# A fused attention and snake-MLP kernel on one core: softmax sums of the first chunk moved from TensorE to VectorE, and new plans for the stages

## The chip, the cores and the metric

The kernel runs on one core of a Trainium2 chip. The metric is the device time of one launch in microseconds (us). Five engines of the core work side by side, each through its own queue in order: TensorE (PE in the profile, with PEld for its weight loads), VectorE (DVE), ScalarE (ACT), GpSimd (POOL) and SyncE (SP), which here issues transfers. They wait for each other by semaphores.

## The reference, cut to what matters

Attention over 8 batches, 12 heads, 448 positions and head size 64, with q and k normalised to unit mean square; its output, laid out as 3584 rows of 768, goes through two matrix products with a "snake" function between them.

```python
q_n, k_n = rmsnorm(q, g_q), rmsnorm(k, g_k)          # q, k, v: (8, 12, 448, 64), float32
scores = (1 / sqrt(64)) * q_n @ k_n.T
attn = exp(scores - max) / (sum(exp) + 1e-9)
x = (attn @ v).transpose(0, 2, 1, 3).reshape(3584, 768)
h = x @ w_in                                         # 768 -> 2048
g = h + sin(alpha * h) ** 2 / alpha
out = g @ w_out                                      # 2048 -> 768
```

## The kernel before

**Stages.** The program is unrolled over the 8 batches; a batch is a stage `b`. A stage first does attention and then the first product (`first_product`, L401). The second product of batch `b - 1` (`quadrants`, L480) is cut into small fillers, which stand in TensorE's queue between the pieces of attention of batch `b`. The last second product stands alone at the end (`whole_array`, L461).

**Chunks.** The 12 heads of a batch are three chunks of four heads: chunk 0, 1 and 2 of stage `b` are `3b`, `3b+1`, `3b+2`. For each chunk, q and k are loaded (L158, L161), squared (`square`: ACT at L262 for the first two chunks, later POOL at L265), summed over the head (`reduce`, DVE, L271), turned into `1/rms` (`rsqrt`, ACT, L280 and L281), multiplied by the gains (`fold_g`, POOL, L268), scaled (`scale`, L290: DVE for chunks 0 to 3 of the whole program, later POOL) and transposed (`pe_transpose` with TensorE at L313 in the first stages, `transpose` by DMA later).

**Scores.** The 448 keys are seven tiles of 64. One `S` makes the scores of one tile for the four heads of a chunk: four 64x64 matmuls that run side by side in the four quarters of TensorE (L335), then one exponential on ScalarE (L338) from the PSUM tile `sc` to a tile `expT` of 128 partitions by 2x448 bf16 in SBUF. A stage has 21 `S`.

**Sums and values.** `attend` multiplies these exponentials with a block of ones ("ones", the softmax sums) and with v ("values", "low", "high"), accumulating over the seven key tiles in PSUM (`av`, L361). Chunk 0 has its own pass, "ones 0" and "values 0", with 64x64 matmuls: per key tile `2 x 2` of them, so 28 for each of the two. Chunks 1 and 2 go together with 64x32 matmuls. After the ones, ScalarE makes the reciprocal as exp(-ln(sum)) in a tile `rec` in SBUF (L366, L367), and VectorE multiplies `av` by it into `xT` (L373).

**First product.** 96 matmuls of 128x128 by 448 columns in eight PSUM tiles of two output blocks each. Each block then goes through ScalarE's sine (L379), a square (POOL at L382 for even blocks, ScalarE at L384 for odd ones) and VectorE's multiply-add into `g_sb` (L387), and only then does its PSUM tile come free.

**Fillers.** One `F` is eight 64x64 matmuls of 384 columns. After 64 of these matmuls VectorE drains the unit with a copy and an add from PSUM (L486, L487), and the PSUM tile comes free.

**Order.** All orders are written out in plans: a string of tokens for the part with attention, a string of PSUM slot numbers, and a dictionary of tasks beside the first product, keyed by its output tile (-1 is early in it, 8 its end). `STAGE_0`, `STAGE_1` and `STAGE_N` (stages 2 to 7) are such plans. Tokens: `S4` is an `S` with four idle matmuls ahead of it, `F` or a number of them fillers of the unit in work, `f` a filler of the unit after it; `o v x y z` are the passes of `attend` (ones 0, values 0, ones 1, low 1, high 1), each for so many key tiles; `q u g r k` are square, reduce, fold_g, rsqrt, scale of the chunk and half named; `p` and `t` are the transposes by TensorE and by DMA, `l V W O` loads of q and k, v, w_in, w_out, and `b` idle matmuls that keep TensorE busy. Tokens only set the order in each engine's queue. There are four PSUM tiles of two banks (`bank_pair`), shared by everything above: a matmul into a slot waits until the slot's former tile has been read.

The tile pools that matter: `expT` 17 buffers, `rec` 2, `xT` 2, `sq` 2 (of the pool `norm`), `snake` 3.

Of the kernel before, what the change touches and what calls it, by code (L numbers as in the profile page):

```python
# [17 lines left out]
try:  # L18
# [5 lines left out]
F32 = mybir.dt.float32  # L24
BF16 = mybir.dt.bfloat16
# [5 lines left out]

STAGE_0 = (
    (
        "L G b11 q00 u00 q01 g0 b15 r00 u01 k00 r01 D1 k01 V00 q11 u11 p00 q10 V02 W11 p011 S4 u10 q20 r1 "
        "g1 S4 q21 S1 l3 u20 S1 k11 k10 S4 u21 S g2 r2 p1 k20 S2 V01 S2 S o3 q30 S W00 W12 k21 l4 o4 D2 "
        "q40 W01 p2 l5 S1 g4 S u30 q31 W02 g3 u40 v1 q41 S v6 u31 S S S3 S1 S3 x2 W10 S S x1 S1 u41 x2 y2 "
        "q51 y3 x2 z1 z1 y2 z1 z1 q50 r4 r3 z2 z1 O00 k31 "
    ),
    "2122130230213212301301321032130132012120312031230",
    {-1: 'u50 k30 u51 O01', 1: 'k401 O10', 2: 'k410 k411', 3: 'O11', 4: 'V10', 5: 'k400', 6: 'D4 l6 V11', 7: 'p3', 8: 'V12 g5 l7 p4'},  # L40
)
STAGE_1 = (
    (
        "q30 6 r2 1 S 4 S 1 S 2 S 2 u30 S k21 1 q41 1 S 1 f S 1 k20 1 S 1 S 1 f 1 S 1 f f f S q31 p2 1 "
        "u31 f l5 S 2 g3 S 2 S r3 2 u41 k30 V10 S 1 q40 1 V11 q50 S o7 v7 1 S k31 1 u40 S 2 S 3 S S 1 x6 "
        "r4 k41 z2 q51 x1 t3 y7 z5 "
    ),
    "13230103120101013131312310202302301230123",
    {-1: 'g4 V12', 1: 'k40', 3: 'u50 g5', 5: 'l6 u51', 8: 't4 l7'},
)  # L50
STAGE_N = (
    (
        "1 r2 q31 q30 f 2 S V10 f 3 V11 f f k20 2 S 3 S 2 k21 S u31 q40 1 t2 1 g3 1 S 1 f u30 S 2 f S f S "
        "r3 q41 f f 1 l5 1 f S 4 u40 S S 5 S S u41 o7 v7 S S 5 S 2 q51 f S 2 S q50 k31 k30 2 S g4 1 u50 S "
        "2 r4 t3 1 S z3 x7 k40 y7 z1 z2 z1 "
    ),
    "01232302102020301301320321310130210231023",
    {-1: 'l6 u51 V12', 1: 'k41', 2: 't4 l7', 3: 'g5'},
)
LAST = "0123012"  # L60

# [1 line left out]
def tokens_of(plan):  # L63

    return [t for word in plan.split() for t in ("F" * int(word) if word.isdigit() else [word])]
# [3 lines left out]
def kernel(  # L69
# [23 lines left out]
    nc = tc.nc  # L93
    B, H, S, D = q.shape
    D_MODEL = H * D
    D_FF = moe_w_in.shape[1]
    P = 128
# [5 lines left out]
    NJ = S // REST  # L103
    assert P == 2 * REST == 2 * D
    NC = NP // 2
# [10 lines left out]
    npool = ctx.enter_context(tc.tile_pool(name="norm", bufs=2))  # L116
    tpool = ctx.enter_context(tc.tile_pool(name="qkT", bufs=8))
    epool = ctx.enter_context(tc.tile_pool(name="expT", bufs=17))
    rpool = ctx.enter_context(tc.tile_pool(name="rec", bufs=2))
    xpool = ctx.enter_context(tc.tile_pool(name="xT", bufs=2))  # L120
    gpool = ctx.enter_context(tc.tile_pool(name="g", bufs=1))
    spool = ctx.enter_context(tc.tile_pool(name="snake", bufs=3))
    opool = ctx.enter_context(tc.tile_pool(name="osb", bufs=3))
# [9 lines left out]
    def bank_pair(name, dtype=F32):  # L133
        slot = int(upcoming.popleft())
        free_at.remove(slot)
        ps = psum.tile([P, 2, 2048 // mybir.dt.size(dtype)], dtype, tag=f"ps{slot}", name=name)
        slot_of[id(ps)] = slot
        return ps

    def give_back(ps):  # L140
        free_at.append(slot_of.pop(id(ps)))
# [3 lines left out]
    def strip(c, pp, hi):  # L145

        s = 2 * hi + (pp if c == 1 else 1 - pp)
        return slice(s * 32, s * 32 + 32)
# [38 lines left out]
    ones = const.tile([P, D], BF16)  # L187
# [17 lines left out]
    def spread_g():  # L205

        nc.gpsimd.tensor_mul(g_rows[:, 2], g_rows[:, 0], g_rows[:, 1])
        ps = bank_pair("gps")
        nc.tensor.matmul(ps[:, 0, :D], ones_row, g_rows[:, 2], start=True, stop=True)  # L209
        nc.scalar.copy(gg[:, 0], ps[:, 0, :D])  # L210
        give_back(ps)

    def spread_alpha():

        ps = bank_pair("aps")
        nc.tensor.matmul(ps[:, 0, :MT], small, ident_f32, start=True, stop=True)  # L216
        nc.vector.tensor_copy(alpha_sb[:, :, 0], ps[:, 0, :MT])
        give_back(ps)
        nc.vector.reciprocal(inv_alpha_sb, alpha_sb)
# [13 lines left out]
    def load_w_out(half, part):  # L233
        src = moe_w_out.rearrange("(mt p) d -> p mt d", p=P)
        cols, mts = slice(half * HALF, (half + 1) * HALF), slice(part * MT // 2, (part + 1) * MT // 2)
        nc.gpsimd.dma_start(out=w_out_sb[:, mts, cols], in_=src[:, mts, cols])

    def keep_busy(n, rhs):


        ps = bank_pair("ps")
        for _ in range(n):
            nc.tensor.matmul(ps[:, 0, :rhs.shape[-1]], blank[:, :P], rhs, start=True, stop=True)  # L243
        give_back(ps)

    qkT, expT, xT = {}, {}, {}
# [92 lines left out]
        give_back(sc)  # L339

    avs, recs = {}, {}
    STEPS = {"o": "ones 0", "v": "values 0", "x": "ones 1", "y": "low 1", "z": "high 1"}

    def attend(b, what, tiles=range(NJ)):

        kind, both = what.split()
        both = both == "1"
        if tiles[0] == 0:  # L350
            avs[what] = bank_pair("av")
        av = avs[what]
        for j in tiles:
            for hi in range(2):
                for c in ((1, 2) if both else (0,)):
                    for pp in range(2):
                        r = slice(pp * 64, pp * 64 + 64)
                        o, k = (strip(c, pp, hi), c - 1) if both else (slice(hi * 64, hi * 64 + 64), pp)
                        d = slice(kind == "high", D, 2) if both and kind != "ones" else slice(D // 2 if both else D)
                        w = ones[r, d] if kind == "ones" else vb[b][r, 2 * c + hi, j, d]  # L360
                        nc.tensor.matmul(av[o, k, :S], w, expT[b * NC + c, j][r, hi, :], start=(j == 0), stop=(j == NJ - 1))  # L361
        if tiles[-1] < NJ - 1:
            return
        if kind == "ones":
            rec = recs[both] = rpool.tile([P, 2, S], F32, tag="rec", name="rec")
            nc.scalar.activation(rec, av[:, :, :S], ACT.Ln)  # L366
            nc.scalar.activation(rec, rec, ACT.Exp, scale=-1.0)  # L367
            give_back(avs.pop(what))
        else:
            if b not in xT:  # L370
                xT[b] = xpool.tile([P, KT, S], BF16, tag="xT", name="xT")
            kts = slice(0, 2) if not both else slice(2, KT, 2) if kind == "low" else slice(3, KT, 2)
            nc.vector.tensor_mul(xT[b][:, kts, :], av[:, :, :S], recs[both])  # L373
            give_back(avs.pop(what))
# [135 lines left out]
    def step(b, token):  # L510

        what, n = token[0], [int(x) for x in token[1:]]
        if what == "b":
            keep_busy(int(token[1:]), blank)
        elif what == "G":
            spread_g()
        elif what == "L":
            spread_alpha()
        elif what == "W":
            load_w_in(*n)  # L520
        elif what == "O":
            load_w_out(*n)
        elif what == "V":
            if b + n[0] < B:
                load_v(b + n[0], n[1])
        else:
            ci = NC * b + n[0]
            if ci >= NC * B:
                return
            if what == "l":  # L530
                return load_qk(ci)
            if ci not in norm:
                norm[ci] = norm_tasks(ci)
            st = norm[ci]
            if what == "D":
                nc.gpsimd.tensor_copy(gate, qk[ci][:, 1, 0, 0:1])
            elif what == "q":
                st.square(n[1])
            elif what == "u":
                st.reduce(n[1])  # L540
            elif what == "g":
                st.fold_g()
            elif what == "r":
                st.rsqrt(slice(n[1], n[1] + 1) if n[1:] else slice(0, 2))
            elif what == "k":
                st.scale(n[1], n[2:] or (0, 1))
            elif what == "p":
                st.pe_transpose((0, 1), n[1:2] or (0, 1), act=len(n) > 2)
            elif what == "t":
                st.transpose()  # L550
            else:
                raise ValueError(token)

    UNIT = MT // 2
    for b in range(B):
# [4 lines left out]
        tiles = deque((b * NC + c, j) for c in range(NC) for j in range(NJ))  # L560
        upcoming.extend(slots)
        done = {what: 0 for what in STEPS}
        for x in tokens_of(plan):
            if x in "Ff":
                fill(x == "f")
            elif x[0] == "S":
                scores(*tiles.popleft(), int(x[1:] or 0))
            elif x[0] in STEPS:
                n = int(x[1:] or 1)
                attend(b, STEPS[x[0]], range(done[x[0]], done[x[0]] + n))  # L570
                done[x[0]] += n
# [36 lines left out]
```

The softmax here doesn't subtract the row's maximum and nothing guards it: scores larger than these inputs give would overflow.

## Time and profile before

| | |
|---|---|
| median of 3 runs | 416.8 us (416.65 to 417.06) |
| profiled execution, first to last instruction | 414.8 us, granted clock 1.00 |
| stage 0 ends (last L401) | 57.7 us |
| stage 1 ends | 105.5 us |
| each of stages 2 to 7 | 47.3 us (for example 200.44 to 247.75) |
| second product of the last batch and last stores | from 389.8 us on |

In a stage of 47.3 us the attention part with its fillers takes 29.0 us and the first product 18.3 us. In the table of groups, each row has the line, the engine, the operation with output and inputs, the number of instructions, then the busy time of the group, the mean duration of one instruction in ns, and the idle time of the engine just before them with what ended it. [...] TensorE starts the next one much earlier, so the busy time of a group of matmuls, and not the mean times the count, is what it costs.

### The profile page before, as it was taken

Reading aid. Unit: us, or ns where it says so; the run is one execution under the profiler, and the core shown is the slowest. Engines: PE = TensorE matmul, PEld = TensorE weight load, DVE = VectorE, ACT = ScalarE, POOL = GpSimd, SP = SyncE. Lnnn points to the kernel's source line nnn. Section 1 sums busy time; section 2 is a strip of 40 time slices with the busy share of each in tenths; the row PEclk is TensorE's granted clock in tenths of the full one; section 3 lists DMA queues with packets and bytes.
Section 4 is the critical chain, followed back from the end, with each engine's and each line's share of the span. In section 5 each row is a group of like instructions: output and inputs, shape, how many; then the busy total and the mean of one; then the engine's idle time right before and its main releaser. Section 6 shows DMA issues by size and latency. Waiting matters only on the chain.

```text
span 414.8 us, 14996 instructions
## 1 busy us (share of the span) xinstructions
PE 403.4 (97%) x6657; PEld 238.9 (58%) x6657; DVE 227.2 (55%) x335; ACT 316.8 (76%) x465; POOL 285.0 (69%) x269
## 2 busy tenths in 40 slices
PE   4999999999999999999999999999999999999995
PEld 2344567655666557655666557655676556665563
DVE  2783774737754565655674565564565464435512
ACT  3698788968888689868889679878889688887600
POOL 3998998898869679498786879697794884003300
PEclk9999999999999999999999999999999999999999
DMA  8999999776273645567294744645375611320022
GB/s 257 176 220 241 168 226 217 167 155 174 29 206 93 150 134 103 158 90 193 70 182 112 175 136 88 172 111 149 92 135 162 89 45 44 82 60 2 1 77 76
DMA packets 64901, 54.07 MB, mean 130 GB/s; under 512 B 36276, under 2 KB 60612, under 8 KB 64836
## 3 DMA queue, kind: packets, MB, share of 16 engines
q1 hardware_dynamic: 51378, 39.60, 36.2%
q0 software_dynamic: 12512, 11.81, 19.3%
q10 hardware_dynamic: 946, 1.70, 1.1%
q8 instruction: 52, 0.85, 0.9%
q14 instruction: 13, 0.11, 0.1%
HBM read 45.62 MB, written 11.01 MB: 137 GB/s over the span
## 4 chain that ended last, share of the span: by engine, by line
PE 94%; ACT 3%; DMA 1%; issue 0%; DVE 0%; POOLq 0%
PE hps L401 35%; PE ops L480 30%; PE av L361 13%; PE sc L335 7%; PE ops L461 5%; ACT expT L338 3%; PE ps L243 2%; DMA small<-in_moe_alpha_dram 1%; PE sc L331 1%; PE tp L313 1%; ACT rec L367 0%; ACT rec L366 0%; PE aps L216 0%; DVE osb L466 0%; PE gps L209 0%
## 5 line engine op out<-in xcount | busy, mean ns | idle before, releaser
L338 ACT ACTIVATE expT<-sc 128x896 bf16<-128x896 f32 x168 | 144.6, 918 | 15.7 <-PE sc L335 15.1
L401 PE MATMUL hps<-xT,w_in 128*128 128x448 bf16 x768 | 146.7, 353 | 0.0
L480 PE MATMUL ops<-w_out_sb,g_sb 64*64 64x384 bf16 x3072 | 146.5, 323 | 0.0
L401 PEld LDWEIGHTS <-w_in 128*128 128x128 bf16 x768 | 74.4, 98 | 71.7 <-issue 3.0
L387 DVE SCALAR_TENSOR_TENSOR g_sb<-s,inv_alpha_sb,hps 128x448 bf16<-128x448 f32 x128 | 81.1, 677 | 62.8 <-POOL s L382 62.4
L480 PEld LDWEIGHTS <-g_sb 64*64 64x64 bf16 x3072 | 89.8, 107 | 39.4 <-issue 2.5
L382 POOL TENSOR_TENSOR s<-s 128x448 f32<-128x448 f32 x64 | 59.4, 932 | 66.9 <-ACT s L379 43.9
L379 ACT ACTIVATE s<-hps,alpha_sb 128x448 f32<-128x448 f32 x128 | 74.5, 626 | 38.4 <-PE hps L401 34.7
L265 POOL TENSOR_TENSOR sq<-qk 128x896 f32<-128x896 f32 x44 | 73.4, 1677 | 29.0 <-DMA qk<-in_k_dram 27.9
L290 POOL TENSOR_TENSOR qkn<-qk,inv 128x448 bf16<-128x448 f32 x80 | 72.8, 938 | 4.2 <-ACT inv L281 2.0
L335 PE MATMUL sc<-qkT 64*64 64x448 bf16 x672 | 57.1, 352 | 0.4 <-DVE qkT L320 0.2
L486 DVE COPY osb<-ops 128x384 f32<-128x384 f32 x48 | 26.7, 557 | 50.3 <-PE ops L480 50.3
L268 POOL TENSOR_TENSOR qk<-qk,gg 128x896 f32<-128x896 f32 x24 | 50.2, 2091 | 2.2 <-ACT g_sb L262 2.2
L271 DVE TENSOR_REDUCE ms<-sq 128x14 f32<-128x896 f32 x44 | 47.0, 1078 | 8.0 <-POOL sq L265 8.0
L373 DVE TENSOR_TENSOR xT<-av,rec 128x896 bf16<-128x896 f32 x24 | 25.4, 1088 | 33.7 <-ACT rec L367 33.7
L384 ACT ACTIVATE s<-s 128x448 f32<-128x448 f32 x64 | 36.9, 577 | 3.0
L361 PE MATMUL av<-expT,vb 64*32 64x448 bf16 (+1 forms) x1120 | 36.8, 350 | 0.1
L335 PEld LDWEIGHTS <-qkT 64*64 64x64 bf16 x672 | 20.2, 107 | 13.4 <-issue 4.5
L487 DVE TENSOR_TENSOR osb<-osb,ops 128x384 f32<-128x384 f32 x48 | 26.6, 554 | 1.7
L361 PEld LDWEIGHTS <-vb 64*32 64x32 bf16 (+1 forms) x1120 | 19.2, 96 | 13.2 <-issue 2.7
L361 PE MATMUL av<-expT,ones 64*32 64x448 bf16 (+1 forms) x672 | 25.3, 350 | 0.2 <-ACT expT L338 0.2
L461 PE MATMUL ops<-w_out_sb,g_sb 128*128 128x384 bf16 x128 | 21.0, 326 | 0.0
(48 smaller groups left out, 185.6 us busy)
## 6 DMA issues: line engine op xcount, KB each, us to landing
out_dram<-osb SPq DMA_DIRECT2D x39, 192.0 KB, 3.1
qk<-in_q_dram SPq DMA_DIRECT2D x16, 448.0 KB, 4.6
qk<-in_k_dram SPq DMA_DIRECT2D x14, 448.0 KB, 4.9
qk<-in_q_dram SPq DMA_DIRECT2D x16, 224.0 KB, 4.1
qk<-in_k_dram SPq DMA_DIRECT2D x16, 224.0 KB, 5.0
vb<-in_v_dram POOLq DMA_DIRECT2D x16, 224.0 KB, 4.4
w_out_sb<-in_moe_w_out_dram POOLq DMA_DIRECT2D x4, 768.0 KB, 12.8
out_dram<-osb SPq DMA_DIRECT2D x26, 96.0 KB, 3.6
```

The costliest lines, as they stand in the source:

```text
L265: nc.gpsimd.tensor_mul(st.sq[w], qk[ci][:, w], qk[ci][:, w])
L268: eng.tensor_mul(qk[ci][:, 0], qk[ci][:, 0], gg.to_broadcast([P, 2 * NJ, D]))
L271: nc.vector.reduce_sum(st.ms[:, w, :], st.sq[w], axis=AX.X)
L290: eng.tensor_mul(n[:, :, hi, :], x[:, hi], inv[:, hi].unsqueeze(2).to_broadcast([P, NJ, D]))
L335: nc.tensor.matmul(sc[pp * 64:pp * 64 + 64, hi, :S], qkt[r, 1, j * REST:(j + 1) * REST], qkt[r, 0, :], start=True, stop=True)
L338: nc.scalar.activation(expT[c, j], sc[:, :, :S], ACT.Exp, scale=SCALE)
L361: nc.tensor.matmul(av[o, k, :S], w, expT[b * NC + c, j][r, hi, :], start=(j == 0), stop=(j == NJ - 1))
L379: nc.scalar.activation(s1, hps, ACT.Sin, scale=alpha_sb[:, m, :])
L382: nc.gpsimd.tensor_mul(s2, s1, s1)
L387: nc.vector.scalar_tensor_tensor(g_sb[:, m, (b % 2) * S:(b % 2 + 1) * S], s2, inv_alpha_sb[:, m, :], hps, op0=ALU.mult, op1=ALU.add)
L401: nc.tensor.matmul(ps[:, m % 2, :S], w_in_sb[m * 2 // MT][:, kt, m % (MT // 2) * P:(m % (MT // 2) + 1) * P], x[:, kt, :], start=(kt == ORD ...
L480: nc.tensor.matmul(st["ps"][os, r, :HALF], g_sb[rs, m, c0 + o * 64:c0 + o * 64 + 64], w_out_sb[rs, m, half * HALF:(half + 1) * HALF], star ...
```

## The change

**What it does.** From stage 1 on, the exponentials of chunk 0 are no longer summed over the seven key tiles by TensorE. VectorE adds the seven `expT` tiles in float32 into the tile that later holds the reciprocal (token `a`, `add_tile`, six additions a stage, all operands in SBUF). The sum is split into two bf16 parts, a rounded copy and the rest (token `i`, `split_sum`: one copy from float32 to bf16 and one subtraction). TensorE then multiplies the ones with the two parts in place of seven tiles: 8 matmuls for 28. Its aim is to take work from TensorE. Stage 0 has no such tokens and sums as before.

**What goes with it.** All three plans are new orders. In stage 0 the first squares stand ahead of the gains' copy on ScalarE, the half k goes first through reduce and scale, 4 idle matmuls stand for 26 at the start, and the transposes of chunk 3 (`p3`) stand in stage 0's attention part and no longer beside its first product. In stages 2 to 7 the scaling of chunks 3 and 4 (`k30 k31 k40 k41`), one square (`q51`) and two reductions (`u50`, `u51`) stand beside the first product. `xT` has one buffer, and a pool `parts` holds the two bf16 tiles.

```diff
+    hpool = ctx.enter_context(tc.tile_pool(name="parts", bufs=1))
-    xpool = ctx.enter_context(tc.tile_pool(name="xT", bufs=2))
+    xpool = ctx.enter_context(tc.tile_pool(name="xT", bufs=1))
...
+    presums = {}
+    def add_tile(b):
+        if b not in presums:
+            presums[b] = SimpleNamespace(n=0, t=rpool.tile([P, 2, S], F32, tag="rec", name="rec"))
+        s = presums[b]
+        first = expT[b * NC, 0] if s.n == 0 else s.t
+        s.n += 1
+        nc.vector.tensor_add(s.t, first, expT[b * NC, s.n])
+    def split_sum(b):
+        s = presums[b]
+        s.parts = [hpool.tile([P, 2, S], BF16, tag=f"part{i}", name="part") for i in range(2)]
+        nc.vector.tensor_copy(s.parts[0], s.t)
+        nc.vector.tensor_sub(s.parts[1], s.t, s.parts[0])
...
+        pre = presums.get(b) if what == "ones 0" else None
+        last = 1 if pre else NJ - 1
...
-                        nc.tensor.matmul(av[o, k, :S], w, expT[b * NC + c, j][r, hi, :], start=(j == 0), stop=(j == NJ - 1))
+                        x = pre.parts[j] if pre else expT[b * NC + c, j]
+                        nc.tensor.matmul(av[o, k, :S], w, x[r, hi, :], start=(j == 0), stop=(j == last))
...
-            rec = recs[both] = rpool.tile([P, 2, S], F32, tag="rec", name="rec")
+            rec = recs[both] = pre.t if pre else rpool.tile([P, 2, S], F32, tag="rec", name="rec")
...
 STAGE_0
-        "L G b11 q00 u00 q01 g0 b15 r00 u01 k00 r01 D1 k01 V00 q11 u11 p00 q10 V02 W11 p011 S4 u10 q20 r1 "
+        "L q01 u01 q00 G b4 g0 u00 D1 V00 r01 W00 r00 k01 k00 q10 u10 q11 l3 u11 p011 r1 p00 S3 k11 S g1 "
...
 STAGE_N
-        "1 r2 q31 q30 f 2 S V10 f 3 V11 f f k20 2 S 3 S 2 k21 S u31 q40 1 t2 1 g3 1 S 1 f u30 S 2 f S f S "
-        "r3 q41 f f 1 l5 1 f S 4 u40 S S 5 S S u41 o7 v7 S S 5 S 2 q51 f S 2 S q50 k31 k30 2 S g4 1 u50 S "
-        "2 r4 t3 1 S z3 x7 k40 y7 z1 z2 z1 "
+        "2 f f 2 S f 4 S 1 a 1 r2 1 k21 S 1 S 2 k20 3 f a S S 2 f f S 1 a t2 a f S 1 q31 q30 1 S 1 a 2 S "
+        "2 S a 2 S 2 f S g3 l5 f f S f u31 f S i 1 q41 1 S 2 o2 1 v3 S v3 v1 S 5 u30 S 1 S V11 u41 q40 S "
+        "1 q50 1 y4 x7 u40 r3 y3 z7 r4 g4 "
-    {-1: 'l6 u51 V12', 1: 'k41', 2: 't4 l7', 3: 'g5'},
+    {-1: 'u50 V10 k31 k30', 0: 'q51', 1: 't3', 2: 'u51 k41', 4: 'l6 V12', 5: 'k40', 6: 't4', 8: 'l7 g5'},
```

## The prediction

> **What bounds the kernel now.** I read the table of engines first, then the chain of waits, then the stages by windows.
>
> ```profile
> PE 403.4 (97%) x6657; PEld 238.9 (58%) x6657; DVE 227.2 (55%) x335; ACT 316.8 (76%) x465; POOL 285.0 (69%) x269
> ...
> PE 94%; ACT 3%; DMA 1%; issue 0%; DVE 0%; POOLq 0%
> ```
>
> TensorE is busy for 97% of the span and makes 94% of the chain that ended last. Since the busy time of pipelined matmuls alone is weak proof, I checked it in the chain by time, for one stage of 47.3 us (200.44 to 247.75):
>
> ```profile
> 200.44 1.42 PE ops L480 x32
> 201.87 0.19 PE sc L335 x4
> 202.06 2.60 PE ops L480 x64
> ...
> 216.03 2.65 PE av L361 x56
> 218.68 0.38 PE sc L335 x8
> ```
>
> Each piece starts where the last ended, and the rates are steady: eight filler matmuls 0.325 us (2.60 / 8), four score matmuls 0.19 us. So from stage 2 on TensorE waits for nobody, and only fewer or shorter matmuls, or a new wait, change a stage. The room of the other engines is in the windows of attention (200.44 to 229.42) and first product (to 247.75):
>
> ```profile
> core 0: us, PE busy (x) PEld busy (x) DVE busy (x) ACT busy (x) POOL busy (x), PEclk, DMA share, GB/s
> ...
> 200.44:229.42 28.98, 28.98 (x758) 19.43 (x757) 15.90 (x25) 26.00 (x36) 22.41 (x19) 1.00 0.51 107
> 229.42:247.75 18.33, 18.33 (x108) 9.37 (x104) 11.11 (x16) 13.07 (x22) 14.39 (x15) 1.00 0.68 175
> ```
>
> VectorE is free for 13.1 us of the attention part, ScalarE for 3.0 and POOL for 6.6. The start is different:
>
> ```profile
> 7.00 8.33 PE L243 MATMUL ps<-blank 128*128 128x512 bf16 x26
> ...
> 10.36 2.21 DVE L290 TENSOR_TENSOR qkn<-qk,inv 128x448 bf16<-128x448 f32 x4
> ...
> 15.26 0.69 PE L313 MATMUL tp<-ident,qkn 64*128 64x64 bf16 x28
> ```
>
> The first transposes need `qkn`, ready at 12.57, but stand behind 26 idle matmuls that end at 15.33. The first exponential starts at 17.43, and from there ScalarE's exponentials bound stage 0 until 37.4; TensorE reaches the first product at 39.43.
>
> [...] The trace of before can't show it: there each late VectorE instruction takes at most one tensor from SBUF (L373, L387, L487 read PSUM beside it), and the times are flat, L387 668 to 683 ns and L382 922 to 946 ns. [...] L373 has 1088. [...] the first 11 matmuls of L243 took 4.82 us (0.44 each), the next 15 took 3.40 (0.23).
>
> **The change, part by part.**
>
> 1. Ones of chunk 0. 56 matmuls of L361 (ones and values) take 2.65 us, 47.3 ns each. 20 of 28 go: 0.95 us a stage. All are on the path. Seven stages: **-6.6 us**, and a stage of 46.36 us.
>
> 2. VectorE's new work: six additions at 1.09 (row L373), one subtraction 1.09, one copy to bf16, priced by L320 (896 elements, 0.62) with 1.09 as upper end: 8.25 us a stage. Attention: 15.9 + 8.25 less two reductions of 1.08 moved to the first product = 22.0 of 28.0 us. It fits by sum. By order: additions wait for exponentials, and behind them stand the drains of fillers (1.1 us each), which free PSUM slots. I follow a stage from its start by the queues: fillers and scores at the rates above put the seven scores of chunk 0 at 2.0, 3.8, 4.9, 5.4, 7.6, 7.8 and 9.3 us; the exponentials (0.82 to 0.92 each, after the table load) end at 4.1, 5.3, 6.7, 7.5, 9.1, 9.9, 10.8. VectorE then goes nearly without a gap: add 5.35 to 6.45, drain to 7.55, three adds to 10.9, drain to 12.1, add, drain, add to 15.4, reduce, copy and subtract to **18.1**. TensorE's queue reaches the new ones at 18.35. So by durations alone it is just hidden, with 0.25 us in hand. I take **0**, and keep the upper end for the rival below. ScalarE's logarithm waits for these ones, not TensorE.
>
> 3. POOL beside the first product: four L290 pairs (8 x 0.94), a square 1.68, a gain 2.09, eight squares of the snake (0.93 each) and two loads (about 2.0) are 20.7 us in 18.3. TensorE needs the slot of output tile 0 at 9.1 us into the product, of tiles 1, 2, 3 each 2.3 later; by POOL's order they come free at about 7.9, 10.5, 11.2, 14.2. The rest runs into the next stage's fillers, whose last blocks are ready at 21.1 and asked for at 21.7. Hidden, **0**, with about 0.6 to 2 us in hand.
>
> 4. `xT` with one buffer: its next write comes some 20 us after its last reader. `parts` and `rec`: their old readers are a stage back. Values 0 holds chunk 0's `expT` until 19 to 21 us; the 18th exponential, which needs the first of them, comes at about 21. **0**.
>
> 5. Stage 0. With squares ahead of the gains' copy, ScalarE can start when the first q and k land, at 5.3 (issued at 0.75, 4.5 to 4.8 to landing), not at 7.21. VectorE's reduces start at 7.06, when alpha is done, not 8.20; with the scaling in its queue next (4 x 0.55) `qkn` is complete at 11.4. TensorE transposes at once. VectorE does two reduces of chunk 1 first (to 13.5), then copies `qkT` (0.7), so scores go at 14.3 and the first exponential at about 14.9: 2.5 us earlier. After the last score, 21 groups of eight `av` matmuls follow (before 18, at 0.21): 0.6 us back. First product about 1.9 us earlier, at 37.5. The 28 transposes of chunk 3 move into time in which TensorE waits for ScalarE: 0.72 us (half of the 1.44 at 57.77) off the path. Late weights: the last ones are issued at about 36.4 and needed at 47; 6 to 9 us to landing before. **-2.5 us**; from 0 [...] to -3.3.
>
> Sum: 416.8 - 6.6 - 2.5 = 407.7; for waits inside thin margins (2 and 3) I add 0.1 us a stage: **408.4 us**.
>
> **The rivals.**
>
> [...] POOL works through exactly the window of the additions: four L290 (3.8 us), two squares (3.4), a gain (2.1) between 5.9 and 15. 8.25 us of VectorE and 9.2 of POOL don't fit in the 13 us between first add and new ones. With VectorE first wherever both wait, the subtraction ends at about 20.8, TensorE stands for 2.5 us in each of seven stages: 407.7 + 17.2 = **425 us**, slower. If they take strict turns, it ends at about 24.6 and TensorE stands for 6.2: 451. Against it: [...] no row of this trace.
>
> POOL becomes the bound. If VectorE never waits but POOL does, POOL needs 36.8 (its busy time in the 47.3 us stage) + 8.25 = 45.1 of 46.36 us, with transfers to wait for on top (5.8 us of waiting for `in_k` in this stage before). Slots beside the first product then come late, and the stage falls back to about 47.3: 416.8 - 2.5 = **414.3 us**.
>
> The start gains nothing. Four idle matmuls in place of 26 leave TensorE at half rate into the first scores, and the loads take most of the DMA engines' time in stage 0 (share 0.84 to 1.13). Then only part 1 counts: **410.2 us**. Against it: scores at half rate (about 0.4 us) still fit beside exponentials of 0.82.
>
> **How the numbers follow.** My forecast has 0.50, the start without gain 0.10, POOL as bound 0.08, [...]. The forecast and the start are faster; POOL as bound is faster in half its cases, the rest split between same and slower: faster 0.64, same 0.02, slower 0.34. I keep the likeliest as the predicted time. The range goes from 405.5 (part 5 at its best, and no waits) up to 428, [...]; what is above it, and a little below, is under 2 in 10.
>
> **What would show it.** Right: stages 2 to 7 of 46.4 us in the chain, still all TensorE; L361 with ones at 64*64 in 84 matmuls (28 in stage 0, 56 later) for 224; additions of about 1.09 us each; POOL's L290 still 0.94; the first exponential near 15. Wrong: additions or POOL's L290 and L265 with long or scattered times, TensorE waiting for `part` before the new ones of L361 or for a slot at L401, or a stage over 47.3 us. My forecast falls if the additions take much more than 1.1 us beside POOL.

## The result, and the profile after

The changed kernel takes **447.4 us** (median of 4 runs, 445.72 to 448.78) against 416.73 before (416.27 to 417.06): ratio 1.0735, interval 1.0685 to 1.0785. It is 30.7 us slower; the forecast was 408.4 us.

(Line numbers are those of the kernel named; they shift by a few from one to the next.) From the profile of the changed kernel: the table of engines, the shares of the chain that ended last, and some groups (line, engine, operation, output and inputs, number | busy us, mean ns | idle before).

```profile
PE 405.4 (91%) x6492; PEld 245.4 (55%) x6495; DVE 312.1 (70%) x391; ACT 318.6 (72%) x465; POOL 312.9 (70%) x269
...
PE 68%; DVE 16%; POOL 5%; issue 4%; DMA 4%; ACT 2%; DVEq 0%; POOLq 0%
...
L266 POOL TENSOR_TENSOR sq<-qk 128x896 f32<-128x896 f32 x44 | 84.5, 1933 | 32.0 <-DVE ms L272 31.3
L291 POOL TENSOR_TENSOR qkn<-qk,inv 128x448 bf16<-128x448 f32 x80 | 85.6, 1095 | 24.0 <-ACT inv L282 17.7
...
L353 DVE TENSOR_TENSOR rec<-rec,expT 128x896 f32<-128x896 f32 x35 | 53.4, 1525 | 1.5
```

The same squares and scalings of POOL before the change:

```profile
L265 POOL TENSOR_TENSOR sq<-qk 128x896 f32<-128x896 f32 x44 | 73.4, 1677 | 29.0 <-DMA qk<-in_k_dram 27.9
L290 POOL TENSOR_TENSOR qkn<-qk,inv 128x448 bf16<-128x448 f32 x80 | 72.8, 938 | 4.2 <-ACT inv L281 2.0
```

TensorE has some 160 matmuls fewer and yet is busy for 405.4 us where it was 403.4. It makes only 68% of the chain, which was 94% before; VectorE now has 16% of it. The additions (L353) take 1525 ns each on average, not 1.09 us. And POOL's instructions, of which not one was changed, became longer: the squares 1933 ns (1677 before), the scaling 1095 (938 before). POOL is 27.9 us busier with the same 269 instructions.

Durations of VectorE's new lines (min/median/max in ns, then first and last start), and below them what TensorE waited for (us in total, times, longest):

```profile
L353 DVE TENSOR_TENSOR rec<-rec,expT x35: 1075/1614/1947, 70.2 to 387.1; 128x896 f32<-128x896 f32 x35
L360 DVE CAST part<-rec x7: 620/1514/1523, 82.1 to 388.2; 128x896 bf16<-128x896 f32 x7
L361 DVE TENSOR_TENSOR part<-rec,part x7: 1093/2447/2451, 82.7 to 388.9; 128x896 bf16<-128x896 f32 x7
```
```profile
PE ops L503 <- DVE osb L510: 11.3, 7, 5.4
PE av L384 <- DVE part L361: 10.5, 5, 2.1
...
PE ops L503 <- DVE g_sb L410: 3.1, 1, 3.1
```

The minima are the unblocked times (1.08, 0.62, 1.09). Two waits of TensorE are new and large: the new ones of L384 wait for the subtraction, and the fillers of L503 wait for a slot whose drain (L510) stands behind an addition in VectorE's queue. The third, 3.1 us for `g_sb`, comes once, between stages 1 and 2; the experiments give its cause.

Why the durations are long is seen in the timeline of one stage (its fillers start at 217.9). Lines of POOL, then VectorE, then TensorE; start, length, engine, line, number merged into the row:

```profile
223.49 5.76 POOL L291 TENSOR_TENSOR qkn<-qk,inv 128x448 bf16<-128x448 f32 x4 [1.81 <-ACT inv L282]
229.22 5.01 POOL L266 TENSOR_TENSOR sq<-qk 128x896 f32<-128x896 f32 x2
...
225.10 5.10 DVE L353 TENSOR_TENSOR rec<-rec,expT 128x896 f32<-128x896 f32 x3
236.09 1.51 DVE L360 CAST part<-rec 128x896 bf16<-128x896 f32 x1
237.64 2.45 DVE L361 TENSOR_TENSOR part<-rec,part 128x896 bf16<-128x896 f32 x1
...
231.31 0.85 PE L503 MATMUL ops<-w_out_sb,g_sb 64*64 64x384 bf16 x16 [0.99 <-DVE osb L510]
240.15 0.38 PE L384 MATMUL av<-part,ones 64*64 64x448 bf16 x4 [2.10 <-DVE part L361]
241.70 0.65 PE L336 MATMUL sc<-qkT 64*64 64x448 bf16 x4
242.07 1.77 PE L384 MATMUL av<-expT,vb 64*64 64x448 bf16 x16
```

Three additions take 5.10 us and lie beside POOL's four scalings, which take 5.76 for 3.6. Both engines are "busy", but each stands for a part of its own instruction. The additions, copy and subtraction of this stage sum to 13.0 us (1.09, 1.61, 1.64, 1.64, 1.51, 1.51, 1.51, 2.45) where the forecast had 8.25. The subtraction ends at 240.09, which is 22.2 us into the stage; the forecast said 18.1. TensorE waits 2.10 us for it, and then runs at half rate: the piece after the four score matmuls starts 0.37 us after their start (242.07 less 241.70; each is recorded for longer, and their row has 0.65), where it was 0.19 before, and the granted clock is 0.50 from 242 to 244 us.

From the start of one first product to the next, in us (the interval 0-1 holds the attention of stage 1, and so on):

| kernel | 0-1 | 1-2 | 2-3 | 3-4 | 4-5 | 5-6 | 6-7 |
|---|---|---|---|---|---|---|---|
| before | 47.8 | 47.6 | 47.3 | 47.3 | 47.4 | 47.3 | 47.3 |
| after | 55.5 | 56.7 | 50.2 | 51.9 | 51.8 | 50.2 | 47.6 |

The last one, in which POOL has no q and k of a next batch to work on, is nearly as before. The waits of 0.99 and 2.10 us are the same in the intervals 2-3 to 5-6. What parts the 50.2 from the 51.9 us is the clock: after the wait of 2.10 us it stayed at 1.00 in the shorter intervals and fell to 0.50 in the longer ones. What decides this is not shown. Stage 0 did become shorter: the first product starts at 37.14 us (39.43 before).

### The profile page after: what moved, and what is told of

It is laid out like the page before. It is cut to its first block, busy times and chain, and to the rows that moved or that the text cites. A ratio compares the mean times of both kernels' runs of the same rounds, so it can differ in the third digit from the quotient of the medians.

```text
span 444.3 us, 14751 instructions
## 1 busy us (share of the span) xinstructions
PE 405.4 (91%) x6492; PEld 245.4 (55%) x6495; DVE 312.1 (70%) x391; ACT 318.6 (72%) x465; POOL 312.9 (70%) x269
## 4 chain that ended last, share of the span: by engine, by line
PE 68%; DVE 16%; POOL 5%; issue 4%; DMA 4%; ACT 2%; DVEq 0%; POOLq 0%
PE hps L424 33%; PE ops L503 17%; PE av L384 10%; DVE rec L353 7%; PE ops L484 5%; PE sc L336 4%; DVE part L361 3%; DMA w_in<-in_moe_w_in_dram 3%; POOL sq L266 2%; DVE part L360 2%; DVE osb L510 2%; DVE osb L509 1%; DVE ms L272 1%; ACT expT L339 1%; POOL qk L269 1%
## 5 line engine op out<-in xcount | busy, mean ns | idle before, releaser
L503 PE MATMUL ops<-w_out_sb,g_sb 64*64 64x384 bf16 x3072 | 154.6, 329 | 14.4 <-DVE osb L510 11.3
L503 PEld LDWEIGHTS <-g_sb 64*64 64x64 bf16 x3072 | 97.6, 109 | 51.8 <-issue 12.0
L410 DVE SCALAR_TENSOR_TENSOR g_sb<-s,inv_alpha_sb,hps 128x448 bf16<-128x448 f32 x128 | 81.0, 677 | 60.5 <-POOL s L405 59.7
L266 POOL TENSOR_TENSOR sq<-qk 128x896 f32<-128x896 f32 x44 | 84.5, 1933 | 32.0 <-DVE ms L272 31.3
L291 POOL TENSOR_TENSOR qkn<-qk,inv 128x448 bf16<-128x448 f32 x80 | 85.6, 1095 | 24.0 <-ACT inv L282 17.7
L336 PE MATMUL sc<-qkT 64*64 64x448 bf16 x672 | 61.8, 364 | 0.7 <-DVE qkT L321 0.5
L269 POOL TENSOR_TENSOR qk<-qk,gg 128x896 f32<-128x896 f32 x24 | 53.9, 2246 | 2.2 <-ACT gg L211 1.8
L353 DVE TENSOR_TENSOR rec<-rec,expT 128x896 f32<-128x896 f32 x35 | 53.4, 1525 | 1.5
L384 PE MATMUL av<-expT,vb 64*32 64x448 bf16 (+1 forms) x1120 | 42.3, 365 | 0.4 <-issue 0.4
L509 DVE COPY osb<-ops 128x384 f32<-128x384 f32 x48 | 26.5, 551 | 15.0 <-PE ops L503 14.9
L384 PEld LDWEIGHTS <-vb 64*32 64x32 bf16 (+1 forms) x1120 | 22.0, 100 | 13.8 <-issue 3.2
L389 ACT ACTIVATE rec<-av 128x896 f32<-128x896 f32 x16 | 14.7, 917 | 20.3 <-DVE osb L509 10.8
L510 DVE TENSOR_TENSOR osb<-osb,ops 128x384 f32<-128x384 f32 x48 | 26.6, 554 | 1.7
```

The lines of the kernel that those rows point to most:

```text
L266: nc.gpsimd.tensor_mul(st.sq[w], qk[ci][:, w], qk[ci][:, w])
L269: eng.tensor_mul(qk[ci][:, 0], qk[ci][:, 0], gg.to_broadcast([P, 2 * NJ, D]))
L291: eng.tensor_mul(n[:, :, hi, :], x[:, hi], inv[:, hi].unsqueeze(2).to_broadcast([P, NJ, D]))
L336: nc.tensor.matmul(sc[pp * 64:pp * 64 + 64, hi, :S], qkt[r, 1, j * REST:(j + 1) * REST], qkt[r, 0, :], start=True, stop=True)
L353: nc.vector.tensor_add(s.t, first, expT[b * NC, s.n])
L384: nc.tensor.matmul(av[o, k, :S], w, x[r, hi, :], start=(j == 0), stop=(j == last))
```

## The experiments

**The disputed instructions alone, and in pairs.** A small kernel with the shapes of this one: each VectorE instruction alone, then in a row beside a row of POOL's squares or scalings. It computes nothing of the reference. The core of it:

```
for j in range(n):
    nc.vector.tensor_add(acc, acc, e[:, j % 7])   # or another VectorE instruction
for j in range(m):
    nc.gpsimd.tensor_mul(sq, x, x)
```

> Not the reference: only instructions of the forms in dispute, in phases that an instruction of ScalarE separates; VectorE alone, POOL alone, then both. Theory 1 [...]: the add of two SBUF tensors takes 1.09 us alone and, beside POOL's 896-element products (1.68 alone), the two take turns, so that VectorE starts an add only every 2.7 us and POOL's products stretch to about the same; the cast from float32 does the same (0.63 alone); a reduction (1.07) and a multiply-add with one input from PSUM (0.68) keep their times beside POOL, and POOL keeps its own. Theory 2 ([...] the longer additions of the changed kernel have another cause, such as late inputs): every form has the same time beside POOL as alone. Open in theory 1: whether an add with two bf16 inputs gets its turn at all between POOL's back-to-back instructions (one of 6.74 us in stage 1 did not).

Timeline rows, first the float32 addition alone (x4), then beside squares; then the all-bf16 addition, the reduction (L84) and the multiply-add with one PSUM input (L91), each beside squares:

```profile
14.58 4.47 DVE L72 TENSOR_TENSOR acc<-acc,e 128x896 f32<-128x896 f32 x4 [14.58 <-ACT s L69]
53.87 15.01 DVE L72 TENSOR_TENSOR acc<-acc,e 128x896 f32<-128x896 f32 x6 [9.28 <-ACT s L69]
55.58 12.35 POOL L94 TENSOR_TENSOR sq<-x 128x896 f32<-128x896 f32 x5
...
85.18 13.39 DVE L78 TENSOR_TENSOR part<-e 128x896 bf16<-128x896 bf16 x8 [2.03 <-ACT e L67]
87.42 10.01 POOL L94 TENSOR_TENSOR sq<-x 128x896 f32<-128x896 f32 x5
...
112.43 6.69 DVE L84 TENSOR_REDUCE ms<-acc 128x14 f32<-128x896 f32 x6 [0.35 <-ACT acc L66]
114.61 8.72 POOL L94 TENSOR_TENSOR sq<-x 128x896 f32<-128x896 f32 x5
135.18 5.70 DVE L91 SCALAR_TENSOR_TENSOR g<-s,inv,ps 128x448 bf16<-128x448 f32 x8 [1.76 <-ACT s L69]
136.95 8.72 POOL L94 TENSOR_TENSOR sq<-x 128x896 f32<-128x896 f32 x5
```

| VectorE instruction | alone, ns | beside squares, ns | the square then, ns |
|---|---|---|---|
| addition, f32 sum | 1091 | 2450 | 2407 |
| addition, all bf16 | 626 | 1984 | 1940 |
| copy f32 to bf16 | 627 | 1984 | 1940 |
| reduction | 1086 | 1086 | 1681 |
| multiply-add, one PSUM input | 680 | 681 | 1680 |

One addition and one square together need 2.485 us, from the start of one square to the start of the next; alone they need 1.09 and 1.68. They hardly overlap: one turn each, and 2.485 is the sum of 2.77 less 0.29. Beside the shorter scaling (0.936) an addition takes 1.707, close to the 1.61 to 1.64 of the stage above. In such a stream the two engines take strict turns, and the waiting lies inside the duration (2450 ns for 1091, and 2407 for 1680 on POOL). The reduction of one SBUF tensor (1086 ns both times) and the multiply-add with one input from PSUM (680 and 681) keep their times; the copy from float32 to bf16 reads one SBUF tensor too, and is blocked (1984 for 627). What in the chip makes them take turns is not shown. So the flat times of L387 and L382 before the change said nothing about the additions.

**The same work, without the second SBUF input.** Changed kernel, same order; the additions, the copy and the subtraction are replaced by reductions of about the same length, so that the sums are not computed and TensorE multiplies constants.

```diff
-        nc.vector.tensor_add(s.t, first, expT[b * NC, s.n])
+        x = expT[b * NC, s.n].rearrange("p h (a d) -> p (h a) d", d=D)
+        nc.vector.reduce_sum(s.t[:, 0, :2 * NJ], x, axis=AX.X)
...
-        nc.vector.tensor_copy(s.parts[0], s.t)
-        nc.vector.tensor_sub(s.parts[1], s.t, s.parts[0])
...
+            nc.vector.reduce_sum(halves[0][:, 0, :NJ], x[:, 0].rearrange("p (a d) -> p a d", d=D), axis=AX.X)
+            nc.vector.reduce_sum(halves[1][:, 0, :2 * NJ], x.rearrange("p h (a d) -> p (h a) d", d=D), axis=AX.X)
```

> The changed kernel with each addition, the copy and the subtraction replaced by a reduction of as many elements (1.08 us, half of it for the copy) that reads one SBUF tensor; queues, waits and matmuls stay, the sums are left out. Theory 1 [...]: the stalls go; the kernel comes near the sum of the prediction, 407 to 413 us, with stages 2 to 7 at 46.4 to 47.2 us. Theory 2 (VectorE's longer queue ahead of the drains and of the new ones, or the new order): VectorE has as much to do in the same order, so the time stays above 430 us.

413.58 us (412.68 to 415.57), ratio 0.9926 (0.9901 to 0.995): a little faster than before, and 0.6 us above the upper end of what I had expected. From its page and its timeline (starts of first products):

```profile
PE 393.6 (96%) x6495; PEld 237.5 (58%) x6495; DVE 281.6 (69%) x393; ACT 318.1 (77%) x465; POOL 285.6 (70%) x269
```
```profile
107.68 2.15 PE L508 MATMUL ops<-w_out_sb,g_sb 64*64 64x384 bf16 x48 [3.10 <-DVE g_sb L415]
...
228.50 18.34 PE L429 MATMUL hps<-xT,w_in 128*128 128x448 bf16 x96
274.87 18.33 PE L429 MATMUL hps<-xT,w_in 128*128 128x448 bf16 x96
321.23 18.34 PE L429 MATMUL hps<-xT,w_in 128*128 128x448 bf16 x96
```

The stages are 46.36 us (274.87 less 228.50, and again), and POOL's busy time is 285.6 us, as before the change. So VectorE has the time for this much work in this order. What the stand-ins take away, 33.8 of the 447.4 us, is the blocking between VectorE and POOL with all that follows from it. TensorE tells how: against this kernel the changed one is busy for 11.8 us more with the same matmuls (405.4 and 393.6), since it runs slower after some of its stands (granted clock over the span 0.974, here 0.999), and its other time grew from 17.3 to 38.9 us of the span (410.9 and 444.3), which are 21.6 us of standing.

**The new order alone** (changed kernel without `a` and `i`, 28 ones matmuls as before; first part of the diff) and **the new stage 0 alone** (kernel before with the changed `STAGE_0`; second part).

```diff
-        "... 1 a 1 r2 1 k21 ... f S i 1 q41 1 S 2 o2 1 v3 ..."
+        "... 1 1 r2 1 k21 ... f S 1 q41 1 S 2 o7 1 v3 ..."
...
-        "L G b11 q00 u00 q01 g0 b15 r00 u01 k00 r01 D1 k01 V00 q11 u11 p00 q10 V02 W11 p011 S4 u10 q20 r1 "
+        "L q01 u01 q00 G b4 g0 u00 D1 V00 r01 W00 r00 k01 k00 q10 u10 q11 l3 u11 p011 r1 p00 S3 k11 S g1 "
```

> The changed kernel's orders, without the additions: tokens a and i left out, ones of chunk 0 by TensorE over seven tiles. Theory 1 [...]: about 6.6 us more than the one-input kernel at most, 414 to 419 us. Theory 2 (the order, above all POOL's work beside the first product, makes the waits): well above 425 us.

> The kernel before with the changed kernel's stage 0 alone. In the changed kernel stage 0 starts its first exponential at 14.5 us for 17.4 and its first product at 37.1 for 39.4, loses 0.5 us to late weights and takes 28 transposes out of the time after it. Theory: the start's part of the prediction holds and this gains 1.5 to 2.7 us (414 to 415.3 us). Rival: the hand-over to the old stage 1 (later fillers' inputs, later loads) eats it, 416.0 to 417.5 us.

The order: 419.56 us (418.61 to 419.98), ratio 1.0047 (1.0029 to 1.0065). That is 0.6 us above what I had expected, and below the 425 us of an order that makes the waits. Its later stages are 47.31 us, as before, but the interval 1-2 is 52.2, with the wait of 3.1 us for `g_sb` that the changed kernel and the last experiment have too. It is a wait for a PSUM slot: the new string of slots of stage 1 ends in 1, so the last output tile of its first product has slot 1, and that of stage 2 begins with 1, so the first filler asks for the same slot at once. It goes on at 107.11 us, right after the last multiply-add that reads that tile (L410, to 107.05). POOL is not what is late: its last two squares of the snake have 1.3 us of idle time each before them. With the old stage 1, whose string ends in 0123, the wait is 1.0 us (experiments below). The new stage 0: 415.18 us (414.94 to 415.48), ratio 0.9952 (0.9934 to 0.9971), as expected.

**The additions in the old order.** The float32 form of the change in the orders of before, and then cheaper forms of it, with the new stage 0 and no additions in stage 1: six additions into one bf16 tile, three pairs added by POOL, the same three by VectorE.

```diff
+        "... S a 1 f u30 S a 2 f S a f S "                              # STAGE_N of before
+        "a r3 q41 f f 1 l5 1 f S a 4 u40 S S i 5 S S u41 o2 v7 ..."
...
-            presums[b] = SimpleNamespace(n=0, t=rpool.tile([P, 2, S], F32, tag="rec", name="rec"))
+            presums[b] = SimpleNamespace(n=0, t=hpool.tile([P, 2, S], BF16, tag="part0", name="part"))
...
+            nc.gpsimd.tensor_add(t, expT[b * NC, 2 * s.n], expT[b * NC, 2 * s.n + 1])   # pairs; or nc.vector
```

> The additions, the copy and the subtraction in float32 as in the changed kernel, but put into the queues of the kernel before (all three stages in the old order). [...] the additions cost by themselves, in whatever order: each is beside a POOL instruction and takes 1.6 to 2.5 us in place of 1.09, L291 of POOL 1.7 in place of 0.94, TensorE waits for part before the new ones; 425 to 450 us, of the size of the changed kernel's 447. Rival, the new order of stages 1 to 7 is what costs (0.5 to 1 us a stage and some 5 us from stage 1 to 2 were seen with the order alone): the old order takes that away and the result is 410 to 418 us.

> Stage 0 in the new order, all others in the old one; from stage 2 on the exponentials of chunk 0 are added by six all-bf16 additions into one bf16 tile, and only four ones matmuls in place of 28 remain (six stages). Stage 1 as before. The sum is rounded to bf16 after each addition, so it is a little coarser than the reference asks of the float32 sum. If VectorE were free: 415.2 (stage 0 alone) less 24 x 47.3 ns x 6 stages = 6.8, so 408.4 us. [...] each addition is 0.63 us alone and 2.0 beside a POOL square, and holds POOL for 0.63 at most, so the six end some 8 us later than unblocked at worst and POOL gets some 3.8 us later; the new ones would come late by 0 to 3 us a stage: 409 to 425 us, and far below the 447 of the float32 form, since no copy and no subtraction stand in line after the last addition.

> As the last one, but three additions of pairs of tiles (0+1, 2+3, 4+5), done by POOL itself, so that nothing of VectorE reads two tensors of SBUF; 16 ones matmuls in place of 28 in six stages. [...] no turn is taken, POOL's L291 and squares stay at 0.94 and 1.68, and the gain is 12 x 47.3 ns x 6 = 3.4: 411.8 us, if POOL has the 3 x 0.9 to 1.9 us to spare. Rival, POOL is what has no room, whoever takes its time: stages come to 48 us or more, and the result is 417 to 422 us, with TensorE waiting for g_sb or for slots.

> The same three pairs, added by VectorE. [...] none depends on another: [...] each takes up to 2.0 us and POOL loses up to 1.9 us a stage, but the last addition ends before the new ones are asked for: 411.8 to 413.5 us. If the additions cost nothing but their own time, 411.8; if POOL is so tight that 1.9 us more a stage is too much, 417 or more.

| form, old order | us | ratio (interval) | stages 2 to 6 |
|---|---|---|---|
| six f32, copy, subtraction | 480.13 | 1.1505 (1.1475 to 1.1535) | 58.0 |
| six all-bf16 | 452.77 | 1.0855 (1.0827 to 1.0883) | 54.7 to 55.0 |
| three pairs on POOL | 441.79 | 1.0574 (1.0538 to 1.0611) | 51.7 to 53.1 |
| three pairs on VectorE | 439.03 | 1.0517 (1.0449 to 1.0586) | 50.5 to 53.6 |

All are slower, and lie well above what I had put down for them (but for the open end of the last): I had worked with the length of the turns and not with their place. Stage 7, where POOL has nothing of a next batch, takes 47.1 to 48.8 us in all four. The new order isn't the culprit; it is the better one for additions, which the rival of the first of these expectations had the other way round. In the kernel with six all-bf16 additions, VectorE's timeline of one stage, then TensorE's, then the sum of this wait over the kernel:

```profile
221.35 2.68 DVE L355 TENSOR_TENSOR part<-expT 128x896 bf16<-128x896 bf16 x1
...
226.48 5.54 DVE L355 TENSOR_TENSOR part<-part,expT 128x896 bf16<-128x896 bf16 x3
231.94 0.55 DVE L511 COPY osb<-ops 128x384 f32<-128x384 f32 x1
...
233.12 0.96 PE L336 MATMUL sc<-qkT 64*64 64x448 bf16 x8 [5.58 <-DVE osb L512]
...
PE sc L336 <- DVE osb L512: 27.9, 5, 5.6
```

The three additions (5.54 us for 1.9) lie beside POOL's gain (2.09 alone) and two squares, its longest instructions, and the drains that TensorE needs stand behind them: 5.58 us of waiting in a row. The pairs on POOL leave VectorE out of it and lose as much, and there TensorE waits for the pairs themselves:

```profile
L351 POOL TENSOR_TENSOR part<-expT x18: 1862/1866/1883, 114.8 to 379.0; 128x896 bf16<-128x896 bf16 x18
...
PE av L386 <- POOL part L351: 15.8, 10, 1.7
```

Three of them are 5.6 us a stage, and the stages are 5.0 to 6.4 us over the 46.7 that the missing matmuls would give, though POOL was busy for only 36.8 of 47.3 us before. Its idle time is not where it could be used: in one stage of this run POOL works without a gap from 210.3 to 239.3 us, and then idles for 6.2 us (242.9 to 249.1) around the start of the first product, after the pairs and the ones that need them.

**The additions in the new order.** Places as in the changed kernel, stage 1 of before without additions: six all-bf16; three pairs; the float32 form of the change (`e11_old_stage1` in the expectations); and that with a last addition that writes one bf16 tile, so that copy and subtraction go. The first part of the diff is common to all four, the second is the last one's; the forms of the first two are those of the experiments above.

```diff
-        "q30 4 q31 S r2 4 S S 2 u30 2 S 1 k20 a 1 S f f S 1 u31 a 2 S 1 k21 1 S a 2 S 2 S 1 q41 p2 S f f "
+        "q30 6 r2 1 S 4 S 1 S 2 S 2 u30 S k21 1 q41 1 S 1 f S 1 k20 1 S 1 S 1 f 1 S 1 f f f S q31 p2 1 "
...
-        nc.vector.tensor_add(s.t, first, expT[b * NC, s.n])
+        out = s.t
+        if s.n == NJ - 1:
+            out = hpool.tile([P, 2, S], BF16, tag="part0", name="part")
+            s.parts = [out]
+        nc.vector.tensor_add(out, first, expT[b * NC, s.n])
```

> The six all-bf16 additions (and four ones matmuls) at the places that the changed kernel gives its additions, in its order of stages 2 to 7; stage 0 new, stage 1 old and without additions; no copy, no subtraction. [...] against the changed kernel each pair of turns is 0.46 us shorter and the 4.0 us of copy and subtraction are gone from the line before the new ones, 6.8 us in all where the stages lost 3.8 to 5.5 us: the last addition ends before TensorE asks; what stays is POOL's delay of 6 x 0.63 = 3.8 us a stage. 408.4 us if POOL has that room in this order, up to 425 if it has not. Rival, the place of the additions doesn't matter, only their number and kind: 452 us as with the same additions in the old order.

> Three all-bf16 additions of pairs at the places of the first, third and fifth addition of the changed kernel, 16 ones matmuls; otherwise as the last one. [...] 411.8 us (415.2 less 12 x 47.3 ns x 6) if three turns fit, with POOL late by 1.9 us a stage; by the rival about 439 us as in the old order.

> The changed kernel with stage 1 of the kernel before (no additions in stage 1, 28 ones matmuls there), all else as changed. Stage 1 with its hand-over to stage 2 cost 52 to 56 us in the changed kernel against 47.3: if that is stage 1's own doing, the result is 447 less 8 to 13 us, 434 to 440; if the loss only moves on to stage 2, about 445.

> As e11_old_stage1 (437.24 us), but the sixth float32 addition writes one bf16 tile, of which TensorE takes the ones in four matmuls; copy and subtraction are left out. What of the loss is the six float32 additions (and POOL's turns behind them), what the copy and subtraction in line after them? If the line before the new ones is what counts: the copy (1.5 us beside POOL) and the subtraction (2.45) go from a chain that makes the stages 51.9 where 46.2 are wanted; stages of about 48, 414 to 420 us. If POOL's delay by the additions counts (6 x 1.1 us a stage with them, 1.7 more with copy and subtraction): stages of about 50, 428 to 432 us. If neither counts any more, 410 us as with the all-bf16 additions.

| form, new order | us | ratio (interval) | intervals 2-3 to 5-6 |
|---|---|---|---|
| six f32, copy, subtraction | 437.24 | 1.0467 (1.0431 to 1.0504) | 50.2 to 51.9 |
| six f32, the last to bf16 | 419.55 | 1.0064 (1.0047 to 1.0081) | 47.6 to 48.2 |
| three pairs, bf16 | 414.67 | 0.9937 (0.9914 to 0.996) | 46.7, once 47.4 |
| six all-bf16 | **410.33** | 0.9832 (0.98 to 0.9864) | 46.2 |

The last two of these expectations were met in one of their readings, the all-bf16 form came 1.9 us above its better figure, and the pairs 2.9 us above theirs. Going up this ladder and on to the changed kernel: float32 in place of bf16 additions costs 9.2 us; the copy and subtraction 17.7, of which about 1.1 are four more ones matmuls a stage (at 47.3 ns); stage 1 in its new form 10.2 (the two intervals that it touches go from 48.4 and 53.1 to 55.5 and 56.7). In stage 1, TensorE's wait of 5.4 us behind one addition (last section) and the 3.1 in place of 1.0 us for slot 1 are the largest pieces that the waits show. The three steps are by their making the whole way from 410.3 to 447.4; each is the cost at its place in the ladder.

The kernel with six all-bf16 additions is the fastest here, 7.0 us below before; its sum is rounded to bf16 after each addition. Page, then VectorE and POOL in one stage:

```profile
PE 393.5 (96%) x6491; PEld 240.1 (59%) x6491; DVE 256.2 (63%) x371; ACT 317.6 (78%) x465; POOL 295.0 (72%) x269
...
PE 94%; DVE 2%; DMA 1%; ACT 1%; issue 1%; POOL 0%; POOLq 0%; DVEq 0%; ACTq 0%
```
```profile
249.60 0.63 DVE L355 TENSOR_TENSOR part<-expT 128x896 bf16<-128x896 bf16 x1
251.72 3.26 DVE L355 TENSOR_TENSOR part<-part,expT 128x896 bf16<-128x896 bf16 x3
...
250.11 4.39 POOL L291 TENSOR_TENSOR qkn<-qk,inv 128x448 bf16<-128x448 f32 x4 [1.80 <-ACT inv L282]
```

The same three additions that took 5.54 us in the old order take 3.26 here: their partners are POOL's short scalings, and the first addition starts before POOL does. TensorE's wait of 5.6 us is gone. TensorE has 94% of the chain again. Alone, too, the all-bf16 addition is the shorter one: 626 ns against 1091 in the small kernel.

## Why the prediction was wrong

- **Step 1, the ones: held.** The forecast stage of 46.36 us was measured as 46.36 with the stand-ins.
- **Step 2, VectorE's new work: this is the step that failed**, in its words "I take **0**, and keep the upper end for the rival". Its durations were right for VectorE alone (1.09, 0.62, all seen as minima). The sum beside POOL is 13.0 us in place of 8.25, and the subtraction ends 22.2 us into the stage in place of 18.1. With 0.25 us in hand, TensorE stood for 0.99 and 2.10 us in each of the stages 3 to 6, which came out 3.8 to 5.5 us over the forecast 46.36. The signs named for "wrong" are there: long and scattered additions, longer L291, TensorE waiting for `part`, stages over 47.3 us.
- **The rival that came true** is the one in which VectorE's additions and POOL's work do not fit side by side. I gave it 0.32 (two thirds of that for about 425 us or less), with "no row of this trace" against it; it was then an assumption, which neither a trace nor a run had shown. The trace of before could not speak on it, since VectorE's late instructions there take at most one tensor from SBUF; that a trace has no example of an effect is no evidence against it. Its two forms were 425 and 451 us. The turns are mostly strict (2.485 us for an addition and a square in the small kernel), the form behind the 451. That 447.4 lies so near to 451 is in part luck: the subtraction came at 22.2 and not at 24.6 us, as most partners were the short scalings, so the stages 3 to 6 lost 3.8 to 5.5 us and the last one 1.2, where the rival's sum had 6.2 for each; what it left out made up for that.
- **Missing in the rival's sum** were the slower TensorE after some of the stands (11.8 us), and stage 1 with its hand-over, where the losses were largest (intervals 0-1 and 1-2, 9.2 and 10.3 us over 46.36).
- **Step 3, POOL beside the first product: 0 held** in the later stages. Between stages 1 and 2 the order alone cost 4.9 us (52.2 for 47.3), 3.1 of them the wait for slot 1. I hadn't followed stage 1's string of slots; POOL had no part in that wait.
- **Step 4, buffers: 0** held; the waits of TensorE name no buffer of `xT`, `expT` or `parts` that came free late.
- **Step 5, stage 0: nearly held.** First exponential at 14.50 us (forecast 14.9), first product at 37.14 (37.5), worth 2.07 us alone (2.5), with 0.4 to 0.5 us of waiting for `w_in`. That refutes the rival in which the start gains nothing. TensorE was slow into the first scores, as that rival had it (the first eight of these matmuls took 528 to 579 ns each, the median of all is 349), and the start gained all the same.
- **POOL as the bound** didn't come as I put it (VectorE never waiting). But its core, that POOL has no room where the sums are needed, is what the three pairs on POOL showed for the old order.

The parts that held give 407.7 us; the stand-ins took 413.6. Of these 5.9 us, 5.1 are the intervals 0-1 and 1-2 (48.3 and 49.5 us, for 46.36 each). The other 33.8 are step 2.

## What to carry to other kernels

Before VectorE is given an addition of two SBUF tensors, or a copy within SBUF from float32 to bf16, list what POOL does in the same microseconds, and price each instruction at its own time plus one of POOL's, on both engines (2.77 us for the addition and the square here, where 2.45 was measured). Then make the additions short (bf16 operands: 626 ns alone for 1091), few, and place them before POOL starts or beside its shortest instructions, with nothing that TensorE needs behind them. Durations that grow on both engines at once, with no idle time before them, are the mark of this in a profile (here 1525 ns for 1091 on VectorE, and 1933 for 1677 on POOL). Where the strings of slots of two stages meet, look whether a slot is asked for again at once.

## What was not expected of the hardware

Turns are not always taken one by one. In stage 1 of the changed kernel the first addition, with its inputs ready, took 6.74 us:

```profile
62.56 6.74 DVE L353 TENSOR_TENSOR rec<-expT 128x896 f32<-128x896 bf16 x1
63.10 3.61 POOL L291 TENSOR_TENSOR qkn<-qk,inv 128x448 bf16<-128x448 f32 x4
66.68 1.67 POOL L266 TENSOR_TENSOR sq<-qk 128x896 f32<-128x896 f32 x1
```

POOL ran four scalings and a square at their unblocked times past the waiting addition, although by the profile the addition had started before each of them; so the strict turns of the small kernel do not cover this. The drain behind this addition is the one for which TensorE waited 5.4 us. In the old order the first addition of a stage lost two turns in the same way, again and again (2.68 us all-bf16, 3.14 with the float32 output). All of these are first additions, of two bf16 tiles, that began while POOL was in a run; yet such an addition took its turn after one square in the small kernel (begun 0.05 us after a square of 1.68 us; it and five more took 11.29 us there). What decides it stays open.

A reduction over tiles, with four bf16 tiles 1792 bytes apart summed for 224 columns, took 1664 ns for 896 elements in the small kernel, against 1086 for the float32 reduction along a row. It keeps that time beside squares, and so do they (1.68 us), but it is no cheap way around the additions.
